# Batch 2's x by DMA transpose with its num three groups earlier, and the loads of v, k and q reordered

## The chip, the cores and the metric

The kernel runs on one core of a Trainium2 chip. The metric is device time in microseconds (us). Every run told of here counts as fast: on one core that means within 1.5% of the fastest run of its kernel. A run has a *span* (first to last instruction in the trace) and a *time*; the time is 1.7 to 2.1 us more than the span.

## The reference, cut to what matters

```python
def _attn_ref(q, k, v):                     # (8, 8, 576, 64) each
    q_p, k_p = phi(q), phi(k)               # phi(x) = elu(x) + 1
    kv  = einsum('bhsd,bhse->bhde', k_p, v)
    num = einsum('bhsd,bhde->bhse', q_p, kv)
    den = einsum('bhsd,bhd->bhs', q_p, k_p.sum(axis=2))[..., None] + 1e-06
    return num / den
# x = attention output as (4608, 512)
def _moe_ref(x, w_in, w_out, beta):         # 512 -> 2048 -> 512
    h = x @ w_in
    return (h * sigmoid(beta * h)) @ w_out
```

## The kernel before

Eight batches go through a pipeline. While TensorE does a batch's two dense layers ("H": x times w_in; "Y": g times w_out), the attention of the next batch is put between its matmuls, in groups. A plan says after which group which attention step is issued. Of one batch's attention, TensorE does the kv product, the num products (q_p times kv, one for each tile of 128 rows), and, in early batches, the transposes that x needs before it can enter the first layer. From batch `DMA_T` on, x is transposed by DMA instead.

```python
def num_norm(b, t):                          # VectorE: x = num / den, as xs
    ...
    if by_dma(b) or t == NJ:                 # by_dma: b >= DMA_T (3)
        nc.sync.dma_start_transpose(out=x_dst(b, t), in_=xs...)

def x_trans(b, t, wide=False, dve=False):    # the other way: 4 matmuls and a copy
    tp = tr_bank(wide)...                    # wide: one of the 2 shared "att" buffers
    for p in range(KC):
        nc.tensor.matmul(tp[:, p, :n], xv[:n, p*P:(p+1)*P], identity[:n, :n], is_transpose=True, ...)
    copy(x_dst(b, t), tp[:, :, :n], dve)

# batch 1's second layer, with batch 2's attention in it
y_phase_wide(1, {
    1: [F(phi, 2, 0), F(q_trans_dma, 2), F(phi, 2, 1)],
    6: [F(kv_mm, 2), F(kv_evac, 2), F(held_load, 4, 2)],
    11: [F(num_mm, 2, 0), F(num_norm, 2, 0)],
    12: [F(num_mm, 2, 1), F(num_norm, 2, 1), F(x_trans, 2, 0, wide=True, dve=True)],
    13: [F(num_mm, 2, 2), F(num_norm, 2, 2)],
    14: [F(x_trans, 2, 1, wide=True, dve=True), F(num_mm, 2, 3), F(num_norm, 2, 3)],
})
# ... cut: the loop over b = 2..8, in which
        h_phase(b, ..., groups, plan)
        load_next(b + 3)                     # v, k, q of batch b+3
```

`hold` is a tiny GpSimd copy from a tile: loads issued behind it on GpSimd's queue wait until that tile is written. In the lines of the trace L475 is H's matmul, L527 Y's, L421 num, L362 kv, L455 the transposes of x on TensorE, L407 the DMA transpose to q_pT, L441 that of x.

## Time and profile before

| | before |
|---|---|
| time, median of 3 runs | 293.01 us (292.94 to 293.87) |
| span of the profiled run | 291.3 us, granted clock 0.997 |
| TensorE busy | 97% of the span |
| batch 2's kv product starts | 72.62 us |
| batch 4's kv product starts | 124.85 us |
| last 32 matmuls (L559) start | 283.94 us |

The last rows are starts in TensorE's timeline; the two kv products of the table, as the timeline has them (start, length, what):

```profile
72.62 0.82 PE L362 MATMUL att<-vaug,qk_p 128*64 128x65 bf16 x40
124.85 0.82 PE L362 MATMUL att<-vaug,qk_p 128*64 128x65 bf16 x40
```

### The profile page before, as it was taken

To read this page: it belongs to the slowest core of one execution; us is meant where nothing else is said; L and a number is where in the kernel's file an instruction comes from. 1 tells how busy PE (TensorE), PEld (TensorE's weight loads), DVE (VectorE), ACT (ScalarE), POOL (GpSimd) and SP (SyncE) were. 2 spreads that over 40 slices of the span, in tenths; PEclk is the share of its full clock that TensorE was granted. 3 is DMA by queue.
4 is the path that set the end of the run, shared out by engine and by line. 5 is a ranking of instruction groups with operands and counts; after the bars stand their busy time and mean duration, and the time that the engine had idled before them with its cause. 6 is when DMAs were issued, how large, how long until landed. Compare 5 with 4: busy or idle time off the path is not lost.

```text
span 291.3 us, 4693 instructions
## 1 busy us (share of the span) xinstructions
PE 281.8 (97%) x1875; PEld 142.6 (49%) x1895; DVE 119.2 (41%) x239; ACT 173.5 (60%) x228; POOL 50.7 (17%) x73
## 2 busy tenths in 40 slices
PE   8889999999999999999999999999999999999994
PEld 3466445644574544455444544454445444444444
DVE  3874387504384265426441645163616400110012
ACT  2888788889987762877177708780760077017500
POOL 8923574100605100510041000000000000000000
PEclk9999999999999999999999999999999999999998
DMA  8999999994899986798379955032503400120033
GB/s 149 197 207 344 258 275 193 257 161 79 107 200 227 185 152 108 121 177 152 103 114 171 158 105 116 2 90 90 126 2 84 116 36 0 52 94 1 0 73 73
DMA packets 73590, 37.55 MB, mean 129 GB/s; under 512 B 41168, under 2 KB 68064, under 8 KB 73568
## 3 DMA queue, kind: packets, MB, share of 16 engines
q0 software_dynamic: 38912, 20.19, 48.5%
q1 hardware_dynamic: 34464, 16.92, 24.8%
q8 instruction: 15, 0.25, 0.4%
q10 hardware_dynamic: 192, 0.14, 0.2%
q14 instruction: 7, 0.06, 0.1%
HBM read 36.71 MB, written 9.44 MB: 158 GB/s over the span
## 4 chain that ended last, share of the span: by engine, by line
PE 82%; DMA 9%; POOL 4%; DVE 2%; issue 1%; ACT 1%; POOLq 0%; DVEq 0%
PE mm L527 37%; PE mm L475 37%; DMA xqk<-in_moe_w_out_dram 5%; DMA g<-in_moe_w_out_dram 4%; PE att L421 3%; PE att L362 2%; POOL xqk L135 1%; PE mm L559 1%; PE att L475 1%; POOL w_in L162 1%; DVE qk_p L242 1%; POOL vraw L135 1%; ACT q_pT L387 1%; DVE xs L437 0%; PE att L395 0%
## 5 line engine op out<-in xcount | busy, mean ns | idle before, releaser
L467 ACT ACTIVATE g<-mm,beta_c 128x512 bf16<-128x512 f32 (+2 forms) x156 | 97.2, 632 | 87.5 <-PE mm L475 87.2
L527 PE MATMUL mm<-w_out,g 128*128 128x512 bf16 x542 | 126.6, 379 | 1.2 <-issue 0.3
L475 PE MATMUL mm<-xT,w_in 128*128 128x512 bf16 (+2 forms) x560 | 107.9, 349 | 0.6 <-DVE xT L385 0.5
L475 PEld LDWEIGHTS <-w_in 128*128 128x128 bf16 x656 | 62.2, 98 | 61.6 <-DMA w_in<-in_moe_w_in_dram 0.6
L527 PEld LDWEIGHTS <-g 128*128 128x128 bf16 x560 | 53.2, 98 | 58.9 <-issue 0.3
L537 DVE COPY y_sb<-mm 128x512 f32<-128x512 f32 x27 | 18.7, 692 | 72.9 <-PE mm L527 69.4
L229 ACT ACTIVATE e<-xqk 128x2560 bf16<-128x2560 bf16 x14 | 31.9, 2328 | 0.1
L242 DVE TENSOR_TENSOR qk_p<-r,e 128x2560 bf16<-128x2560 bf16 x14 | 20.8, 1490 | 12.8 <-ACT e L229 12.1
L437 DVE TENSOR_TENSOR xs<-att,rden 128x512 bf16<-128x512 f32 x36 | 24.9, 692 | 1.2
L372 DVE CAST kv_bd<-att 64x260 bf16<-64x260 f32 x14 | 6.0, 427 | 33.0 <-PE att L362 32.9
L435 DVE TENSOR_SCALAR den<-att 128x8 f32<-128x8 f32 x36 | 5.9, 163 | 29.5 <-PE att L421 29.2
L72 POOL DMA_DIRECT2D vraw<-in_v_dram x7 | 6.4, 917 | 65.1 <-DVE vaug L385 61.1
L421 PEld LDWEIGHTS <-q_pT 128*128 128x128 bf16 (+1 forms) x160 | 10.7, 100 | 9.7 <-DVE xs L437 1.9
L421 PE MATMUL att<-kv_bd,q_pT 128*128 128x130 bf16 (+1 forms) x160 | 14.3, 222 | 0.8 <-DVE kv_bd L385 0.4
L475 PE MATMUL mm<-xT_tail,w_in 128*128 128x512 bf16 x63 | 13.9, 379 | 0.1
L237 DVE TENSOR_SCALAR r<-xqk 128x2560 bf16<-128x2560 bf16 x14 | 11.4, 820 | 3.9 <-DMA xqk<-in_q_dram 2.4
L608 PE MATMUL mm<-g 128*128 128x512 bf16 x29 | 9.3, 477 | 1.3 <-DVE g L145 1.2
L229 ACT ACT_TABLE_LOAD x7 | 9.0, 1283 | 0.1
L436 DVE RECIPROCAL rden<-den 128x8 f32<-128x8 f32 x36 | 7.3, 203 | 1.2
L72 POOL DMA_DIRECT2D xqk<-in_k_dram x7 | 6.9, 984 | 3.0 <-DMA w_in<-in_moe_w_in_dram 1.5
L475 PE MATMUL att<-xT,w_in 128*128 128x512 bf16 x32 | 7.2, 379 | 0.0
L72 POOL DMA_DIRECT2D xqk<-in_q_dram x7 | 6.3, 904 | 3.9 <-ACT w_out L214 2.0
(77 smaller groups left out, 134.6 us busy)
## 6 DMA issues: line engine op xcount, KB each, us to landing
out_dram<-y_sb SPq DMA_DIRECT2D x28, 256.0 KB, 2.3
xqk<-in_k_dram POOLq DMA_DIRECT2D x7, 512.0 KB, 9.5
xqk<-in_q_dram POOLq DMA_DIRECT2D x7, 512.0 KB, 11.0
vraw<-in_v_dram POOLq DMA_DIRECT2D x7, 512.0 KB, 11.6
w_in<-in_moe_w_in_dram POOLq DMA_DIRECT2D x4, 512.0 KB, 10.3
g<-in_moe_w_out_dram POOLq DMA_DIRECT2D x4, 512.0 KB, 10.7
out_dram<-y_sb SPq DMA_DIRECT2D x14, 128.0 KB, 5.2
xqk<-in_moe_w_out_dram POOLq DMA_DIRECT2D x2, 512.0 KB, 14.4
```

The costliest lines, as they stand in the source:

```text
L72: eng.dma_start(out=dst[:, :, 0:NJ, :].rearrange("p h j d -> p h (j d)"), in_=src[b, :, 0:MAIN, :].rearrange("h (p j) d -> p h (j d)", j=NJ),)
L229: nc.scalar.activation(st[b, "e", a][:, h0:h1], xqk[b % NX][:, a, h0:h1], ACTF.Exp)
L237: nc.vector.tensor_scalar(st[b, "r", a][:, h0:h1], xqk[b % NX][:, a, h0:h1], 0.0, 1.0, ALU.max, ALU.add)
L242: nc.vector.tensor_tensor(st[b, "p"][:, a].rearrange("p j (h d) -> p h j d", h=H)[:, h0:h1], st[b, "r", a][:, h0:h1], st[b, "e", a][:, h0: ...
L421: nc.tensor.matmul(nps[r0 : r0 + n, p // 2, c0 : c0 + 2 * (D + 1)], st[bb, "qT"][:, t, p, :n], kv_bd[bb % 2][:, p], start=True, stop=True, ...
L436: nc.vector.reciprocal(rden[:n], den[:n])
L437: nc.vector.tensor_mul(xs[:n], nv[:, :, :, 0:D], rden[:n, :, :, None].to_broadcast([n, 2, 4, D]))
L467: nc.scalar.activation(g_sb[b % 2][:, ff, c0:c1], hp[:, c0:c1], ACTF.Silu, scale=beta_c[:, ff : ff + 1],)
L475: nc.tensor.matmul(hp[:, c0:c1], w_in_sb[ff // 4][:, kc, (ff % 4) * P : (ff % 4 + 1) * P], x[:, t0:t1, kc, :] if b < B else x[:, kc, c0:c1 ...
L527: nc.tensor.matmul(yp, g_sb[b % 2][:, ff, t * P : (t + 1) * P], w_out_sb[ff // 4][:, ff % 4, :], start=(ff == 0), stop=(ff == FC - 1),)
L537: nc.vector.tensor_copy(y_sb, yp)
L608: nc.tensor.matmul(st["warm"], g_sb[0][:, FC - 1, 0:P], g_sb[0][:, FC - 1, :], start=True, stop=True, skip_group_check=True,)
```

## The change

The intent is to take batch 2's transposes off TensorE. For x to arrive by DMA in time, num moves from groups 11 to 14 to groups 8 to 11, and batch 2's first layer begins with 8 instead of 4 groups in halves, so that it can start on tiles 0 and 1. To keep the DMA queues free for the transposes, v is loaded in mid-H and k and q are held until x has landed.

```diff
-    DMA_T = 3
+    DMA_T = 2
...
+    def held_v(b, n):
+        if b < B:
+            hold(st[n, "qT"][0:1, NJ, KC - 1, 0:1]); load_v(b)
+    def held_kq(b, n):
+        if b < B:
+            hold(xT[n % 3][0:1, NJ - 1, KC - 1, 0:1]); load_k(b); load_q(b)
...
-            12: [F(v_copy, 2)],
+            12: [F(v_copy, 2), F(load_v, 4)],                   # batch 1's H
...
-        6: [F(kv_mm, 2), F(kv_evac, 2), F(held_load, 4, 2)],    # batch 1's Y
-        11: [num 0], 12: [num 1, x_trans 0], 13: [num 2], 14: [x_trans 1, num 3]
+        6: [F(kv_mm, 2), F(kv_evac, 2)],
+        8: [num 0], 9: [num 1], 10: [num 2], 11: [num 3, F(held_kq, 4, 2)]
...
-            groups = 4 x (0, 2), 4 x (2, 4), ALL[4:]; x_trans of tiles 2 and 3 after groups 0 and 1
+            groups = 8 x (0, 2), 8 x (2, 4), ALL[8:]
-            plan[7 + o] = [F(v_copy, n)]
+            plan[7 + o] = [F(v_copy, n), F(held_v, b + 3, n)]
-        load_next(b + 3)
+            plan[12] = [F(held_kq, b + 3, n)]
```

(The lines on num and groups are shortened here; `load_next` also loses its case for b >= 5.)

More of the change, by code (lines that the diff above doesn't have):

```diff
@@ L586, in load_next @@
         if b < B:
-            if b >= 5:
-                load_v(b)
             load_k(b)
             load_q(b)
-            if b < 5:
-                load_v(b)
+            load_v(b)
     held = consts.tile([1, 1], BF16)
@@ L598, in hold @@
         nc.gpsimd.tensor_copy(held, a)
-    def held_load(b, n):
-        hold(st[n, "qT"][0:1, NJ, KC - 1, 0:1])
-        load_next(b)
+    def held_v(b, n):
+        if b < B:
+            hold(st[n, "qT"][0:1, NJ, KC - 1, 0:1])
+            load_v(b)
+    def held_kq(b, n):
+        if b < B:
+            hold(xT[n % 3][0:1, NJ - 1, KC - 1, 0:1])
+            load_k(b)
+            load_q(b)
     def warm(n):
@@ L737 @@
         1: [F(phi, 2, 0), F(q_trans_dma, 2), F(phi, 2, 1)],
-        6: [F(kv_mm, 2), F(kv_evac, 2), F(held_load, 4, 2)],
-        11: [F(num_mm, 2, 0), F(num_norm, 2, 0)],
-        12: [F(num_mm, 2, 1), F(num_norm, 2, 1), F(x_trans, 2, 0, wide=True, dve=True)],
-        13: [F(num_mm, 2, 2), F(num_norm, 2, 2)],
-        14: [
-            F(x_trans, 2, 1, wide=True, dve=True), F(num_mm, 2, 3), F(num_norm, 2, 3),
-        ],
+        6: [F(kv_mm, 2), F(kv_evac, 2)],
+        8: [F(num_mm, 2, 0), F(num_norm, 2, 0)],
+        9: [F(num_mm, 2, 1), F(num_norm, 2, 1)],
+        10: [F(num_mm, 2, 2), F(num_norm, 2, 2)],
+        11: [F(num_mm, 2, 3), F(num_norm, 2, 3), F(held_kq, 4, 2)],
     })
@@ L752 @@
             groups = (
-                [(ff, 0, 2) for ff in range(4)] + [(ff, 2, 4) for ff in range(4)] + ALL[4:]
+                [(ff, 0, 2) for ff in range(8)] + [(ff, 2, 4) for ff in range(8)] + ALL[8:]
             )
-            plan = {
-                0: [F(x_trans, 2, 2, dve=True)],
-                1: [F(x_trans, 2, 3, dve=True)],
-            }
         o = len(groups) - FC
```

## The prediction

> **What bounds the kernel now.** I read the busy table and the slices first, to see which engine is never free.
>
> ```profile
> PE 281.8 (97%) x1875; PEld 142.6 (49%) x1895; DVE 119.2 (41%) x239; ACT 173.5 (60%) x228; POOL 50.7 (17%) x73
> PE   8889999999999999999999999999999999999994
> PEclk9999999999999999999999999999999999999998
> ```
>
> TensorE is busy in every slice and at full clock. Busy alone proves little, since the ends of matmuls are modelled, so I took rates from the chain of waits, in order of time. Its steady part, here from batch 3's first layer on, is TensorE only:
>
> ```profile
> 113.69 11.22 PE mm L475 x52
> 124.92 0.75 PE att L362 x40
> 125.67 2.70 PE mm L475 x12
> 128.37 0.22 PE mm L527
> 128.58 0.05 issue
> ```
>
> 52 matmuls of 512 columns in 11.22 us are 216 ns each, back to back. So from there on the time is the sum of TensorE's work, and what is taken off TensorE shortens the kernel one for one. The same view shows one place after the start-up in which the chain leaves TensorE: batch 1's second layer, where batch 2's num products are made.
>
> ```profile
> 77.87 0.25 PE att L421 x4
> 78.11 0.02 issue
> 78.14 0.18 DVE den L435
> 78.31 0.02 issue
> 78.34 0.21 DVE rden L436
> 78.55 0.02 issue
> 78.58 0.70 DVE xs L437
> 79.28 0.05 issue
> 79.32 0.40 PE att L455 x4
> ```
>
> Here the first transpose of x (L455) waits for VectorE's normalisation of the tile before it. How long TensorE really stands still is read from starts in TensorE's timeline:
>
> ```profile
> 78.80 0.40 PE L421 MATMUL att<-kv_bd,q_pT 128*128 128x130 bf16 x4
> 79.32 0.40 PE L455 MATMUL att<-identity,xs 128*128 128x128 bf16 x4
> 81.53 0.39 PE L455 MATMUL att<-identity,xs 128*128 128x128 bf16 x4
> 82.06 0.41 PE L421 MATMUL att<-kv_bd,q_pT 128*128 128x130 bf16 x4
> ```
>
> Four num products take 0.24 us of issue (78.80 to 79.04), so the gap to 79.32 is 0.28 us. Four transposes take 0.22 us (81.53 to 81.75), so the gap to 82.06 is 0.31 us: that num product waits for one of the two shared PSUM buffers, which the wide transposes rotate through as well. Together 0.59 us of real standstill. Where a group lacks a record (19 matmuls where the code has 20) I kept the code's count.
>
> **What the Trainium skill says.** (1) "TensorE: Matmul & The Clock Gate", section "Wait — 56ns, not 53.3ns?": warm matmuls start every 55.6 ns at 128 columns and every 215.7 ns at 512. The trace agrees: 0.22 us for four transposes, 216 ns for the wide ones. (2) "Trainium Kernel Development and Optimization", its paragraph on reading a trace: matmul busy time is a bad metric, as matmuls are pipelined. The trace agrees: the form at 512 columns is listed at 379 ns but starts every 216 ns, which is why I count starts. (3) "DMA: Bandwidth & Descriptors", section "Queues, rings and completion order": each DMA engine goes round-robin between the queues that have work, a packet at a time. So a transpose issued by SyncE beside a load isn't put behind all of it but shares with it. The trace fits: the transposes to q_pT land in 4.9 us in the median, and the one at 87.5 us, beside loads, in 5.6; the tail transpose at 54 us, in the middle of the start's loads, took 8.1 against a median of 3.7.
>
> **The change part by part.**
>
> *Transposes off TensorE.* Batch 2's x goes by DMA, as batches 3 to 7 do already. This removes 4 tiles x 4 = 16 transposes: 16 x 55 ns = 0.88 us of TensorE, all of it on the path. It also removes 4 copies from VectorE (4 x 0.42 = 1.7 us), off the path.
>
> *The gaps.* Num moves from groups 11 to 14 to groups 8 to 11. Group 7 ends, with the kv product done at 73.44 us, 8 matmuls later: 73.44 + 8 x 0.216 = 75.17 us for the first num, then one per 4 x 0.216 + 0.24 = 1.10 us: 75.2, 76.3, 77.4, 78.5. VectorE begins 0.44 us after each (77.70 to 78.14 now) and needs 1.1 to 1.2 us, so it ends a tile at about 76.7, 77.9, 79.0 and 80.1. The third num needs the first's PSUM buffer: free at 76.7, wanted at 77.4. The fourth needs the second's: free at 77.9, wanted at 78.5. No transpose competes for the buffers any longer, so both gaps go: 0.59 us.
>
> *More half groups in batch 2's first layer.* Eight groups instead of four are cut in halves, so that the first eight products need only tiles 0 and 1. Columns moved are the same: four matmuls of 256 columns take 0.44 us against 0.43 for half of four of 512. Cost under 0.05 us. Sixteen more weight loads of 98 ns lie under matmuls that start every 109 ns.
>
> *The DMA transposes of x.* Four more on SyncE's queue, 1.19 us of issue each, 2.4 us to landing. They land at about 76.7 + 2.4 = 79.1, 80.3, 81.4 and 82.6. Batch 2's first layer now begins at 83.17 - 2 x 0.22 - 0.59 = 82.1 us and needs tiles 0 and 1 then (1.8 us to spare) and tiles 2 and 3 after 8 half groups, at 85.6 us (3 us to spare).
>
> *Loads.* Batch 4's v goes out at about 56 us, when v's copy for batch 2 ends (55.37 + 0.82), behind the loads for batch 3. Its k and q go out when x tile 3 has landed, at about 82.7 instead of 74.3 us, and land in 8 to 10 us (k of the stream at 92 us took 8.5, q 10.1), so by about 95; their exponentials run at about 97. For later batches v goes behind q_pT, and k and q behind x at about 109 us, landing by 120, wanted at 127. None of these is on the path now, and none is expected on it.
>
> *Sum.* 0.88 + 0.59 - 0.03 = 1.45 us saved, and nothing later gives it back as the rest of the chain is TensorE's own work. 293.0 - 1.45 = 291.55; I say 291.5 us, 0.5% less.
>
> **The rivals.**
>
> *Rival A: q_pT comes late.* Num at 75.2 us needs the transpose to q_pT, issued at 69.16 and landed by 74.06, when its holder copy starts. The old order had 3.6 us of slack at 77.7; the new has 1.1. And v of batch 4 is now in the queue just before. The stretches show when the loads before it drain (columns: busy us of each engine, clock, DMA share, GB/s):
>
> ```profile
> 65.00:66.00 1.00, 1.00 (x6) 0.46 (x5) 0.00 (x0) 0.99 (x2) 0.00 (x0) 1.00 0.96 85
> 66.00:67.00 1.00, 1.00 (x7) 0.47 (x5) 0.00 (x0) 1.00 (x1) 0.00 (x0) 1.00 0.24 22
> 69.00:70.00 1.00, 1.00 (x7) 0.45 (x5) 0.27 (x2) 0.98 (x2) 0.00 (x0) 1.00 0.00 0
> 70.00:71.00 1.00, 1.00 (x6) 0.43 (x5) 1.00 (x1) 1.00 (x1) 0.00 (x0) 1.00 0.69 136
> ```
>
> They drain at about 66 us. One load of 576 KB at the 185 GB/s or so of such stretches is an estimated 3.2 us, so v ends near 69.2, and the transpose's packets begin at 70. It fits, just. If they overlap as at 87.5 us, q_pT lands at 69.16 + 5.6 = 74.8: still in time. Only if it slows as the tail transpose did (8.1 / 3.7 = 2.2 times, to some 10.7 us) is num held, till about 79.9, a stall of 4.7 us: 296 us. I give a stall of over 0.5 us one chance in eight.
>
> *Rival B: x comes late.* If the four transposes take twice as long, tile 1 lands at 82.7 instead of 80.3 and the first layer waits 0.5 us: 292.0. Against it: no load is in flight then, which is what the hold on tile 3 is for.
>
> *Rival C: ScalarE becomes the bound in the 16 half groups.* An activation of 256 columns is listed at 473 ns against TensorE's 437 ns per half group; but six in a row took 2.58 us at 54.2 us, 0.43 each, so it keeps up, and it begins with up to 0.4 us of slack in the four PSUM banks. If it runs at 473 after all, 16 x 0.036 = 0.6 us goes into the slack and some 0.2 us shows.
>
> *Rival D: the saving is worth more.* The loads no longer lie beside the stores and q_pT of the same stretch. But TensorE waits for none of these after 84 us, so calmer DMA queues are worth nothing here.
>
> **Range and chances.** The mechanism fixes 1.45 us within about 0.2. Runs of the kernel before spread over 0.9 us, and rivals A to C add only on the slow side. Predicted 291.5 us; 8 in 10 between 290.9 and 292.5. Faster by over 2% (under 287.2) would need four times the TensorE work that the change removes: 0.01. Slower by over 2% (over 298.9) needs a stall of more than 7 us: 0.02. Within 2%: 0.97.
>
> **What would show each step right or wrong.** Right: no L455 rows for batch 2 (32 narrow transposes left of 48), TensorE's timeline from 75 to 98 us without gaps, batch 2's first layer starting near 82.1 us and its second near 97.0 (98.49 now), and every later row of the chain 1.4 to 1.5 us earlier. Rival A: TensorE's wait list shows L421 waiting for the DMA of q_pT near 75 us. Rival B: L475 waiting for the DMA of xT near 82 or 85 us. Rival C: L475 waiting for ScalarE's activation between 84 and 89 us. The prediction is wrong at its root if rows after 98 us contain a new TensorE wait, or if the chain now ends in another engine's work.

## The result, and the profile after

The changed kernel took 291.85 us in the median of 4 runs (291.76 to 292.05), the kernel before 292.98 beside it (4 runs). The ratio is 0.9957, with a 95% interval of 0.9936 to 0.9977. A ratio here is the mean time of one kernel's fast runs over that of the other's of the same rounds, so it is not quite the ratio of the medians. By the measure of 2% the two are the same; the prediction said 291.5 us and 0.97 for "within 2%".

The chain of waits of the changed kernel, in order of time (start, length, what), over the stretch that changed:

```profile
75.23 0.23 PE att L421 x4
75.46 0.86 PE mm L527 x4
76.33 0.23 PE att L421 x4
...
78.75 3.45 PE mm L527 x16
82.20 11.30 PE mm L475 x84
93.51 0.75 PE att L362 x40
...
96.96 1.73 PE mm L527 x8
```

DVE and L455 are gone: the chain is TensorE's own work without a break. Num comes at 75.2 us where it came at 77.9, the second layer of batch 2 at 96.96 where it came at 98.49. TensorE's waits in the whole run (us in total, times, longest):

```profile
PE mm L612 <- DVE g L145: 1.2, 1, 1.2
PE mm L325 <- DVE qk_p L280: 1.2, 1, 1.2
PE mm L475 <- DMA w_in<-in_moe_w_in_dram: 1.2, 1, 1.2
PE att L421 <- ACT q_pT L387: 0.3, 1, 0.3
```

All four lie in the start-up or in batch 1's stage; none is on a DMA of q_pT or xT. The same two kv products as before:

```profile
72.57 0.82 PE L362 MATMUL att<-vaug,qk_p 128*64 128x65 bf16 x40
123.32 0.82 PE L362 MATMUL att<-vaug,qk_p 128*64 128x65 bf16 x40
```

By pieces, from starts in TensorE's timeline (this profiled run and a second one of the same kernel, beside before):

| piece | before | after | after, again |
|---|---|---|---|
| start to batch 2's kv | 72.62 | 72.57 | 74.20 |
| batch 2's kv to batch 4's kv | 52.23 | 50.75 | 50.74 |
| batch 4's kv to the last 32 matmuls | 159.09 | 159.08 | 159.09 |
| last 32 matmuls to the end of the span | 7.36 | 7.70 | 7.67 |

The second row holds the gain, 1.48 and 1.49 us in the two profiles of the changed kernel, against 1.45 predicted. The third shows that nothing in between gives it back. The first is start-up: the second profile has a wait of 1.9 us for the load of w_in there. The last row was not foreseen: 0.3 us come back at the end (spans are given to 0.1 us, so this row is good to 0.05). One thing got slower without costing time. The DMA's times to landing of q_pT's transposes, first before, then after:

```profile
DMA to landing us min/median/max: 4.8/4.9/5.6
```

```profile
DMA to landing us min/median/max: 4.8/9.8/10.3
```

K and q now run beside four of the six transposes; the first and the last have no loads of k and q near them. The transpose issued at 83.97 us landed when its holder copy started, at 94.43, and num wants it at 98.52. So the margin is 4 us; it was 7 (landed 87.50 + 5.6 = 93.1, wanted at about 100).

### The profile page after: what moved, and what is told of

Same layout as the page of the kernel before. It is cut to its first block, busy times and chain, and to the rows that moved or that the text cites. A ratio compares the mean times of both kernels' runs of the same rounds, so it can differ in the third digit from the quotient of the medians.

```text
span 290.1 us, 4739 instructions
## 1 busy us (share of the span) xinstructions
PE 281.8 (97%) x1895; PEld 144.1 (50%) x1895; DVE 116.7 (40%) x235; ACT 174.0 (60%) x232; POOL 54.3 (19%) x79
## 4 chain that ended last, share of the span: by engine, by line
PE 92%; DMA 3%; POOL 3%; ACT 1%; issue 0%; DVE 0%; POOLq 0%
PE mm L527 42%; PE mm L475 41%; PE att L421 3%; DMA w_in<-in_moe_w_in_dram 3%; PE att L475 2%; PE att L362 2%; POOL xqk L135 1%; PE mm L559 1%; POOL vraw L135 1%; ACT q_pT L387 1%; PE mm L455 0%; PE att L395 0%; PE att L455 0%; DVE xT L385 0%; DVE y_sb L385 0%
## 5 line engine op out<-in xcount | busy, mean ns | idle before, releaser
L527 PE MATMUL mm<-w_out,g 128*128 128x512 bf16 x560 | 128.0, 379 | 0.0
L475 PEld LDWEIGHTS <-w_in 128*128 128x128 bf16 x672 | 63.8, 98 | 60.8 <-DMA w_in<-in_moe_w_in_dram 1.3
L595 POOL COPY held<-xT 1x1 bf16<-1x1 bf16 x4 | 2.0, 509 | 63.6 <-DMA xT<-xs 63.6
L72 POOL DMA_DIRECT2D xqk<-in_q_dram x7 | 7.1, 1021 | 3.9 <-ACT w_out L214 2.1
```

What stands on the lines that cost most here:

```text
L72: eng.dma_start(out=dst[:, :, 0:NJ, :].rearrange("p h j d -> p h (j d)"), in_=src[b, :, 0:MAIN, :].rearrange("h (p j) d -> p h (j d)", j=NJ),)
L475: nc.tensor.matmul(hp[:, c0:c1], w_in_sb[ff // 4][:, kc, (ff % 4) * P : (ff % 4 + 1) * P], x[:, t0:t1, kc, :] if b < B else x[:, kc, c0:c1 ...
L527: nc.tensor.matmul(yp, g_sb[b % 2][:, ff, t * P : (t + 1) * P], w_out_sb[ff // 4][:, ff % 4, :], start=(ff == 0), stop=(ff == FC - 1),)
```

## The experiments

Eleven kernels ran, all with results correct by the reference, in four sets; each set has its own runs of the kernel before. Where a piece is named, "the middle piece" is batch 2's kv to batch 4's kv, 52.23 us before and 50.75 in the changed kernel. Each of these runs has one profile.

### The changed kernel again

> The changed kernel as it is, for the ratio that the parts must add up to. My theory (TensorE's own work and gaps: 0.88 us of transposes and 0.59 us of gaps, less 0.1 us for more half groups) expects 1.4 us less than before, ratio 0.9953. If the median difference of 1.13 us of the first runs is the true one, 0.9961.

Six runs: median 292.68 us (291.77 to 293.84), ratio 0.9972 (0.9947 to 0.9998). The middle piece is 50.74. The runs spread by 2 us, and the profile puts such a spread into the start-up (table above). So the ratio of whole runs can't tell 0.9953 from 0.9961; the pieces can. This run decides nothing alone.

### Num early, transposes still on TensorE

```diff
-        11: [num 0], 12: [num 1, x_trans 0], 13: [num 2], 14: [x_trans 1, num 3]
+        8: [num 0], 9: [num 1], 10: [num 2], 11: [num 3], 12: [x_trans 0], 13: [x_trans 1]
```

> The kernel before with batch 2's num products moved to groups 8 to 11 and x still transposed on TensorE (two tiles after groups 12 and 13, two in the next layer). My theory: the two gaps of 0.59 us go, the 0.88 us of transposes stays: ratio 0.998, and a first layer of batch 2 that begins at about 82.6 us. Rival (the gaps are an artefact of the timeline, or move elsewhere): 1.000.

Ratio 0.9978 (0.9953 to 1.0002), median 292.45 us. The middle piece took 51.60 us (72.35 to 123.95), 0.63 less than before, and the first layer of batch 2 began at 82.27 us. The gaps were real and go with the move of num alone: 0.63 us against 0.59 from starts. What is left to the change of 1.48 is 0.85 us, the 16 transposes of 0.88 less the extra half groups.

### The new loads alone

```diff
+            12: [F(v_copy, 2), F(load_v, 4)],  ...  v, k, q of later batches as in the change
-        6: [F(kv_mm, 2), F(kv_evac, 2), F(held_load, 4, 2)],
+        6: [F(kv_mm, 2), F(kv_evac, 2)],
+                1: [F(x_trans, 2, 3, dve=True), F(held_kq, 4, 2)],       # batch 2's H
```

> The kernel before with the new order of loads alone (v mid-layer, k and q behind x), transposes and num as before. My theory: no load is on TensorE's path, so the time of before, ratio 1.000 within 0.001. Rival (calmer DMA queues are worth something, which would make part of the saving theirs): at least 0.3 us less, ratio 0.999 or under. Also q_pT of batches 4 to 6, which the new order puts beside k and q, should take some 10 us to land instead of 5.

A miss: ratio 1.0109 (1.0078 to 1.014), median 296.86 us. That is slower by 1.1%, under the 2% of the measure but clear of the noise, where I had expected nothing. Lines of SyncE's, GpSimd's and TensorE's timelines of this kernel (start, length, what, and in brackets the idle time before):

```profile
88.16 6.23 SPq L407 DMA_TRANSPOSE q_pT<-qk_p  x1
```

```profile
88.03 1.29 POOL L72 DMA_DIRECT2D xqk<-in_q_dram  x1
```

```profile
103.14 0.56 PE L421 MATMUL att<-kv_bd,q_pT 128*128 128x130 bf16 x4 [2.27 <-DMA q_pT<-qk_p]
```

Batch 3's q_pT went out among batch 4's k and q (k at 86.48), took 14.9 us to land, and num waited 2.27 us for it. The middle piece took 56.34 us (73.28 to 129.62), 4.11 more than before: the wait, and 1.57 us on the eight matmuls behind it, which took 3.46 us instead of 1.89 at a granted clock of a half. In the changed kernel the same transpose goes out at 83.97 us, 4 us sooner, because VectorE normalises x earlier and copies no transposes from PSUM: the product that q_pT is made from ends at 82.25 us there (80.76 + 1.49), at 88.09 here. It also goes out ahead of k (84.49), not behind it, and lands after 10.3 us; with 14.9 it would have been 0.35 us late for num at 98.52. Why it lands sooner there was not tested. So this order of loads is safe only together with the other parts.

### The same loads, k and q behind q_pT instead of x

```diff
-                1: [F(x_trans, 2, 3, dve=True), F(held_kq, 4, 2)],
+                1: [F(x_trans, 2, 3, dve=True)],
+            if b == 2: plan[7 + o] += [hold on batch 3's q_pT, F(load_k, 4), F(load_q, 4)]
```

> The new loads alone, as in the kernel that lost 1.1%, but with batch 4's k and q held until q_pT of batch 3 has landed, instead of x. If that kernel lost its 4 us because q_pT of batch 3 was caught beside k and q (landed after 14.9 us, TensorE waited 2.3 us and then ran at half clock), q_pT lands in about 5 us at 93, there is no wait, and the time is that of before, ratio 1.000. If the new loads cost something elsewhere, the loss stays: 1.01.

Ratio 1.0012 (0.9993 to 1.003), median 293.2 us. The middle piece is 52.23 us (72.59 to 124.82), that of before; the holder copy on q_pT started at 92.38, and TensorE's list has no DMA of q_pT. So the loss of the run above was that one collision. This also answers the rival that calmer queues are worth something: with the collision gone, the new loads are worth nothing.

### The change with the old loads

```diff
-        11: [F(num_mm, 2, 3), F(num_norm, 2, 3), F(held_kq, 4, 2)],
+        6: [F(kv_mm, 2), F(kv_evac, 2), F(held_load, 4, 2)],  ...  load_next(b + 3) after H
```

> The changed kernel with the loads in the old order (batch 4's k, q and v all at 74 us, behind q_pT). My theory, that the new order is there only to keep the queues free for x: the four transposes of x at 77 to 82 us share the DMA engines with the loads and take some 2.2 times as long, tile 1 lands at 83 to 86 instead of 80.3 and the first layer of batch 2 stalls on the DMA of xT by 1 to 4 us: 293 to 296 us. Rival (transposes of one tile are too small to mind): 291.9 us as the changed kernel.

Ratio 1.0172 (1.0153 to 1.0191), median 298.19 us. TensorE's wait, and the DMA issues between 74 and 90 us (count, median us to landing):

```profile
PE mm L475 <- DMA xT<-xs: 4.1, 1, 4.1
```

```profile
xT<-xs SPq DMA_TRANSPOSE x4, 8.4
```

Beside the loads the transposes of x took 8.4 us instead of 2.4, and the first layer waited 4.1 us. This is what the new order of loads is for. The whole loss in the middle piece is 6.39 us (57.14 against 50.75), 2.3 more than the wait; the next run shows where most of that comes from. (Another 0.3 us is a wait for batch 3's q_pT, which went out at 85.36 beside the next three loads and took 19.6 us to land.)

### The change with num left late

```diff
-        8: [num 0], 9: [num 1], 10: [num 2], 11: [num 3, F(held_kq, 4, 2)],
+        11: [num 0], 12: [num 1], 13: [num 2], 14: [num 3, F(held_kq, 4, 2)],
```

> The changed kernel with num left at groups 11 to 14. My theory: xs of tile 1 is ready at about 80.4 us, its DMA transpose lands 2.4 to 3 us later, at 82.8 to 83.4, where the first layer wants it at 82.0: a stall of 0.8 to 1.4 us with L475 waiting for the DMA of xT, so 0.8 to 1.4 us above the changed kernel, 292.6 to 293.2, most of the gain lost. Rival (the move is for PSUM's sake alone and the transposes are fast enough): no stall, ratio 0.996 as the changed kernel.

Ratio 1.0076 (1.0051 to 1.0101), median 295.64 us: right in direction, but 4.0 us lost in the middle piece (54.78 against 50.75), not 0.8 to 1.4. Two things were left out. First, SyncE's queue:

```profile
78.90 1.19 SPq L441 DMA_TRANSPOSE xT<-xs  x1
81.05 0.36 SPq L519 DMA_DIRECT2D out_dram<-y_sb  x1
81.51 1.21 SPq L441 DMA_TRANSPOSE xT<-xs  x1
```

A store of y stands between the transposes in program order. It waits for ScalarE's copy of y, which starts only at 80.44 us (ScalarE is in its exponentials until 79.03, and then loads a table until 80.32), so the second transpose went out at 81.51, though VectorE had finished its xs at 79.97 (79.28 + 0.69). Second, TensorE after the wait (timeline; then the stretches of 1 us: busy us of PE, PEld, DVE, ACT and POOL, granted clock, DMA share, GB/s):

```profile
84.07 13.13 PE L475 MATMUL mm<-xT,w_in 128*128 128x256 bf16 x84 [2.20 <-DMA xT<-xs]
```

```profile
84.00:85.00 1.00, 0.93 (x9) 0.87 (x10) 1.00 (x2) 0.30 (x1) 0.00 (x0) 1.00 0.94 281
85.00:86.00 1.00, 1.00 (x7) 0.72 (x6) 0.97 (x2) 0.74 (x3) 0.00 (x0) 0.55 0.49 137
86.00:87.00 1.00, 1.00 (x7) 0.67 (x5) 1.00 (x2) 0.62 (x2) 0.00 (x0) 0.50 0.94 268
```

After 2.20 us of standstill, and 1 us after the matmuls had resumed, the granted clock fell to a half for 3.4 us (0.75 in the stretch from 88 us, 1.00 from 89 on), and the same 84 matmuls took 13.13 us instead of 11.47: another 1.66 us. The wait and this make 3.86 of the 4.0 us lost. The run of the change with the old loads shows the same 13.13 us, and the same 3.4 us at half clock, after its wait of 4.1; the loads alone show 3.4 us too, after 2.27. So num's move is needed, and each of these waits cost some 1.6 us more than its own length.

### K and q not held

```diff
-            12: [F(v_copy, 2), F(load_v, 4)],
+            12: [F(v_copy, 2), F(load_v, 4), F(load_k, 4), F(load_q, 4)],
-        11: [F(num_mm, 2, 3), F(num_norm, 2, 3), F(held_kq, 4, 2)],
+        11: [F(num_mm, 2, 3), F(num_norm, 2, 3)],
```

> The changed kernel with batch 4's k and q not held but loaded right behind its v at 57 us. This takes the rival of my prediction (q_pT of batch 2 comes late) to a higher dose: the loads then drain at about 75 us instead of 69. q_pT, issued at 69.1, should land after about 10 us, as it does beside loads at 84 us in the changed kernel, at about 79.4, and num, wanted at 75.1, stalls 4.3 us on the DMA of q_pT: about 296 us. If q_pT shares fairly and lands in 5.6 us: no stall, 291.9 us.

Ratio 1.0264 (1.0239 to 1.0289), median 300.58 us: slower by over 2%. The expectation was right in kind, and had half of the loss:

```profile
82.19 0.61 PE L421 MATMUL att<-kv_bd,q_pT 128*128 128x130 bf16 x4 [6.55 <-DMA q_pT<-qk_p]
```

Q_pT of batch 2, issued at 69.52, kept num until 82.19 us: 12.7 us instead of 4.9, a wait of 6.55, and the groups of four matmuls after it ran at 1.91 us instead of 1.02 until 87 us. The middle piece took 60.23 us, 9.48 more than the changed kernel's: the wait, and 2.9 us of slower matmuls (the clock was at a half from 81.1 to 87.9 us, so from 1.1 us before the wait ended). This is the prediction's rival A, made to happen with more loads than it spoke of.

### Whole groups in batch 2's first layer

```diff
-                [(ff, 0, 2) for ff in range(8)] + [(ff, 2, 4) for ff in range(8)] + ALL[8:]
+                ALL
```

> The changed kernel with batch 2's first layer in whole groups. The first product then wants tile 3 at 82.0 us; it lands at about 82.9. Stall 0.9 us on the DMA of xT, less 0.18 us saved on the 64 narrow matmuls that the halves cost: 0.7 us above the changed kernel, 292.6 us. Rival (halves cost more than the wait they hide): at or under 291.9 us.

Ratio 0.999 (0.9972 to 1.0008), median 292.85 us. The middle piece took 51.70 us, 0.95 more than the changed kernel's, against 0.7 expected.

```profile
83.33 11.38 PE L475 MATMUL mm<-xT,w_in 128*128 128x512 bf16 x52 [0.87 <-ACT y_sb L535]
```

The standstill is there. The trace names ScalarE's copy of y, but in the changed kernel the layer starts 1.27 us after these copies begin (82.04 against 80.77), which would be 82.31 here, a microsecond before; and GpSimd's holder copy, which waits for x tile 3, started at 83.30: so I read it as the DMA. The layer up to kv took 11.32 us (83.33 to 94.65) against 11.40 (82.04 to 93.44), so the eight groups in halves cost 0.08 us (0.18 expected), and they hide a wait of 0.9 to 1.0. The kernel before has four groups in halves already, so of the 0.08 an estimated half, 0.04 us, belongs to the change. After this shorter standstill the clock stayed at 1.00.

### A try for more: one of q's two copies on VectorE

```diff
-                st[b, "qT"][:, ts[i] : ts[i] + m, :, :n], tp[:, i : i + m, :, :n], False
+                st[b, "qT"][:, ts[i] : ts[i] + m, :, :n], tp[:, i : i + m, :, :n], i > 0
```

> A try for more: the changed kernel with one of the two copies of batch 1's transposed q from PSUM on VectorE instead of both on ScalarE (1.95 us in a row, for which num waits 0.3 us at 46 us). Expected: that wait goes, 0.2 to 0.3 us less than the changed kernel. Rival: VectorE's copy delays its kv copy by as much, and nothing is won.

Ratio 0.9993 (0.9972 to 1.0013), median 292.47 us: nothing won, and 0.91 us lost in the piece that it was for. That piece, from batch 1's kv to batch 2's, took 29.63 us (43.56 to 73.19) against 28.72 in the changed kernel. The wait for ScalarE's copy became a longer one on the kv copy behind it:

```profile
PE att L421 <- DVE kv_bd L372: 1.0, 1, 1.0
```

VectorE's copy of q started at 44.73 us, when ScalarE's ended (43.67 + 1.02 = 44.69). The two did not run side by side; both write the tile q_pT and read one PSUM tile, and which of the two orders them I did not test. VectorE's kv copy had to wait behind.

### Where the 0.3 us at the end come from

Every kernel so far with batch 2's x by DMA spent 7.59 to 7.70 us from the last 32 matmuls to the end of the span; before, num early, and the two runs of the loads alone spent 7.36 to 7.40.

```diff
 # in the kernel before, in num_norm; x_trans stays and is what is used
+        elif b == 2:
+            nc.sync.dma_start_transpose(out=spare[:, t], in_=xs...)
```

> The kernel before with four DMA transposes of batch 2's x added that nobody reads (TensorE still transposes x for use). It asks whether the 0.3 us that every kernel with batch 2's x by DMA spends more between its last product and its end (7.6 to 7.7 us from the first of the last 32 matmuls to the end of the span, against 7.36 without) comes from the four DMA transposes themselves. If it does: an end of 7.6 us or more, and 0.2 to 0.3 us above before. If not: 7.36 us and the time of before. No stall of TensorE either way.

Ratio 1.0034 (1.0005 to 1.0062), median 293.89 us. The end took 7.66 us (284.34 to 292.0): four transposes that nobody reads bring it about. (Q_pT of batch 3 was later too, and TensorE waited 0.3 us for it, which I had ruled out; the middle piece is 52.70 us.) Then four more, in the changed kernel, late, when the loads are done:

```diff
 # in the changed kernel, ahead of batch 7's second layer
+            for t in range(1, NT):
+                nc.sync.dma_start_transpose(out=spare[:, t - 1], in_=st[7, "xs", t]...)
```

> The changed kernel with four more DMA transposes that nobody reads, late and in a stretch where nothing else uses the DMA queues. The unread ones in the kernel before gave it the longer end (7.66 instead of 7.36 us from the first of the last 32 matmuls). If every DMA transpose adds to the end, the end is now 7.9 us or more. If the end depends on where the last stores fall in a rotation of the queue's completion counters, with a period of eight, it is back at 7.36 us and the kernel 0.3 us faster than the changed one. If it is something of the first four alone, 7.66 us stays.

Ratio 0.9948 (0.9924 to 0.9972), median 291.71 us. The middle piece is 50.74 us (72.81 to 123.55) and the end is back at 7.37 us (282.63 to 290.0). SyncE's wait for the landing of the last stores, in the changed kernel, in the kernel before with four idle transposes, and in the changed kernel with four more:

```profile
SPq L801 <- DMA out_dram<-y_sb: 1.6, 1, 1.6
```

```profile
SPq L809 <- DMA out_dram<-y_sb: 1.6, 1, 1.6
```

```profile
SPq L808 <- DMA out_dram<-y_sb: 1.4, 1, 1.4
```

In the kernel before it was 1.4. Four more transfers on SyncE's queue lengthen the end, eight do not, so it is no cost that each transfer adds. The rotation with a period of eight that the expectation names foretold this, but it is not shown: only the counts 0, 4 and 8 were tried, and the last four of the eight also go out in another place (232.14 us), so count and place are not told apart. SyncE has 11 semaphore events at the end in all of these kernels, so their number is not the cause. This last kernel is also the fastest of all in its profile's pieces, though its runs (291.50 to 292.71 us) overlap with those of the changed kernel.

## Why the prediction was right

*The bound.* Right. From batch 2 on the time is TensorE's work: between batch 4's kv and the last 32 matmuls all three profiles agree within 0.01 us.

*Transposes, gaps and halves.* Right: 1.45 us predicted (its three terms sum to 1.44), 1.48 measured in the middle piece. The gaps came out at 0.63 us (0.59 predicted), and the transposes less the halves at 0.85 (0.85 predicted, 0.88 - 0.03). Of the 0.08 us that eight groups in halves cost, read from whole groups, the four added ones are an estimated 0.04, against 0.03 predicted. TensorE's list has 32 narrow transposes left of 48, as the prediction said.

*Num, x and q_pT in time.* Right, with nearly the times given: num at 75.06 (75.17), the first layer at 82.04 (82.1), the second at 96.79 (97.0). X tile 3 landed at about 83.0, not 82.6, and is wanted at 85.6.

*"Nothing later gives it back".* This step failed for a small term: 0.3 us come back at the end of the span, and the kernel before with four idle transposes shows that they bring it. With it, the span is 1.2 us shorter in the profiled run (291.3 to 290.1), not 1.45, which is most of the distance between the predicted 291.5 and the measured 291.85.

*The loads.* The conclusion held (not on the path), but the reasoning was too light. It had q_pT beside loads land in 5.6 us, read from one transpose that met only the end of a load (v, issued at 77.39, landed after 11.8 us, about 89.2; the transpose went out at 87.50). Issued next to k and q it takes about 10 us in the changed kernel, and 14.9 us in the loads alone, where it cost 1.1%. The change escapes because q_pT goes out 4 us sooner and lands in 10.3 us, neither of which the prediction worked out: that the conclusion held was in part luck.

*The rivals.* None occurred. Rival A and rival B are real: not holding k and q, or keeping the old loads, makes num or the first layer wait 6.55 or 4.1 us. Both were undersized. The waits were longer than the prediction's 4.7 and 0.5 us, though each run puts more loads beside the transposes than the rival supposed; and the slower clock after a standstill was left out. In all, rival A's run lost 9.5 us in the middle piece: 6.55 of wait and 2.9 of slower matmuls. Rival C did not show: ScalarE took the 16 half activations in 6.97 us, 0.44 each, TensorE's own pace. Rival D was right to be dismissed: the loads alone, without the collision, were worth nothing.

## What to carry to other kernels

When an engine is busy back to back, count starts, not busy time: the work removed and the standstills removed then add up to the gain within hundredths of a microsecond. A change that moves work to another queue comes with conditions (here: num early, loads held), and undoing each one alone shows which of them carry it. Before trusting a margin on a DMA, read its landing time beside the very transfers that will run with it, and add to a missed wait on TensorE what the slower clock after it costs: here some 1.6 us after waits of 2.2 to 4.1 us, 2.9 us after one of 6.55, and nothing after 0.9 to 1.0.

## What the Trainium skill lacked or had wrong

- "TensorE: Matmul & The Clock Gate", section "What's actually happening", has the clock fall after at least one idle window of about 3.4 us. Here 2.20 us without a matmul were enough for a half clock of 3.4 us and 1.66 us lost (num left late), and 2.27 us in the loads alone; 0.9 to 1.0 us were not (whole groups).
- "DMA: Bandwidth & Descriptors", section "Queues, rings and completion order", describes the sharing between queues by packets but gives no landing times for it. Here a transpose of one x tile took 8.4 us beside three loads instead of 2.4, and q_pT took about 10 to 14.9 us beside two loads, and 19.6 beside three, instead of 4.9.
- I found no page that has it: the end of a kernel can move with the transfers that its store queue carried long before. Four more made it some 0.3 us longer (7.59 to 7.70 us against 7.36 to 7.40), eight more, four of them late, did not (7.37).
